# Window attention into a SiLU MLP: the first eight pairs' P times V in float32, with V whole in SBUF

## The chip, the cores and the metric

The kernel runs on one NeuronCore of a Trainium2 chip, in one launch. The metric is device time in microseconds (us) of that core. Before the change the median of three runs is 961.42 us (960.21 to 961.59).

## The reference

Eight batches of eight heads, 576 positions, head dimension 64, all in float32. Attention looks back over a window of 128 positions with a linear bias per head; its output, 4608 tokens of 512 features, goes through a SiLU MLP with 2048 hidden features.

```python
scores = scale * np.matmul(q, k.transpose(0, 1, 3, 2))
mask = (rel >= 0) & (rel < window)
scores = np.where(mask, scores + bias[None], -1000000000.0)
scores = scores - np.max(scores, axis=-1, keepdims=True)
attn = np.exp(scores)
attn = attn / (np.sum(attn, axis=-1, keepdims=True) + 1e-09)
out = np.matmul(attn, v)
x = out.transpose(0, 2, 1, 3).reshape(B * S, H * D)
h = x @ w_in
g = h * (1.0 / (1.0 + np.exp(-h)))
y = g @ w_out
```

## The kernel before

Two batches stand one after the other as 1152 rows, nine blocks of 128 (NBLK); there are 36 blocks. A **pair** p is one block i = p // 2 of query rows and one half q = p % 2 of the eight heads, so there are 72 pairs. A block attends to itself and to the block ahead of it (block 0 of a double batch to itself alone). Tokens go through the MLP in nine groups of four blocks (512 tokens); the first group needs the pairs 0 to 7 finished, and all later pairs are worked on while the MLP of an earlier group runs on TensorE.

A pair takes these steps. `scores`: products of q and k into two PSUM tiles (sp). `row_max`: on VectorE, adds the bias table `tab` and takes the row maximum (t, mx). `exps`: exponentials on ScalarE. Transposition of P, for the first eight pairs on TensorE into PSUM (`p_transpose_first`, pt), for later ones by DMA (`p_transpose`, hl from hr). Splitting P, scaled by 2048, into two float16 parts (hl): `p_hi_first` on ScalarE and `p_lo_first` on VectorE. `attend`: P times V (av), where V is split into two float16 parts as well (v1, v2, after multiplication by a power of two), so three products of float16 stand for one. A column of ones in v1 gives the row sum. `normalize` (L525 to L539) divides; for the first four blocks it writes x into float32 tiles (`early`), which `x_transpose` turns on TensorE (xp) and splits into xh (ScalarE) and xl (VectorE).

The power of two by which V is multiplied (`vsc`) comes from the maximum of |V| over the double batch: `vscale_load` fetches nine blocks, `vscale_reduce` takes each block's maximum (odd blocks on VectorE, even ones on ScalarE for the first double batch), `vscale_finish` joins them in three stages: a reduction (vcol), a transposition on TensorE (vt) with a few operations on one element, and a product that spreads the result (vs). `v_hi` and `v_lo` split V; for the first four blocks both run on GpSimd (L384, L392, L393).

The MLP's weights arrive as 64-bit words and are turned into float32 parts in SBUF, 16 slices of each matrix, 32 in all. `w_next_load` issues a slice's load (512 KB). `w_next` splits a slice: two operations on ScalarE (L712, L719), a join on VectorE (L724), a copy on ScalarE (L734), a subtraction on GpSimd (L128), and it orders one further load a step later. AHEAD loads are ordered beforehand. Three slices are split ahead of the MLP, the rest during its first group.

The order on every engine is written by hand: `put(point, fn, ...)` files a function under a step number; step 0 is the first half product of the MLP, and `at(p)` is the step at which pair p's scores stand. Pairs 0 to 7 are eight steps apart, from step -82 to -26. Each engine runs its instructions in that order, and SP issues all DMAs of the kernel in order too: one that waits for its tile holds back those behind it. Tiles with a common tag share memory: `rv` (two buffers) serves the V blocks to be split and the blocks whose maximum is taken for a later double batch; the tags in EARLY are those of late weight slices. `keep_warm(n)` puts n matmuls without a use on TensorE (into the last columns of an av tile).

Of the kernel before, what the change touches and what calls it, by code (L numbers as in the profile page):

```python
# [6 lines left out]
F32 = mybir.dt.float32  # L7
# [60 lines left out]
EARLY = ("w0_15", "w1_15", "w0_14", "w1_14", "w0_12", "w1_12", "w0_13")  # L68
AHEAD = 9
# [15 lines left out]
def tile_window_attention_then_silu_mlp(ctx, tc, qk, qk16, v, w_in, w_out, base8, out):  # L85
# [72 lines left out]

    def vscale_load(b, i):

        t = early_tile(XD + i) if b == 0 else pool.tile([P, DM], F32, tag="rv", bufs=2, name=f"vm{b}_{i}")
        nc.sync.dma_start(t, v[b, i * P : (i + 1) * P, :])
        vred.setdefault(b, {})[i] = t

    def vscale_reduce(b, i):
# [4 lines left out]
        if b == 0 and i < GT:  # L170
            rvs[i] = t

        if b > 0 or i % 2:
            nc.vector.tensor_reduce(m, t, axis=AX.X, op=ALU.max, apply_absolute_value=True)
        else:
            junk = pool.tile([P, DM], F32, tag="gt", name=f"vj{b}_{i}") if b == 0 else t
            nc.scalar.activation(junk, t, AF.Abs, accum_out=m)
# [199 lines left out]
    def load_v(i):  # L377
        b, j = divmod(i, NBLK)
        rvs[i] = pool.tile([P, DM], F32, tag="rv", bufs=2, name=f"rv{i}")
        nc.sync.dma_start(rvs[i], v[b, j * P : (j + 1) * P, :])  # L380
# [7 lines left out]
    def v_lo(i):  # L388
        rv = rvs.pop(i).rearrange("p (h d) -> p h d", h=H)
        if i < GT:  # L390
            vs = pool.tile([P, H, D], F32, tag="gl", name=f"vs{i}")
            nc.gpsimd.tensor_scalar(vs, rv, vsc[0][:, 0:1], 1.0, op0=ALU.mult, op1=ALU.mult)  # L392
            nc.gpsimd.tensor_sub(v2[:, i % VSLOTS], vs, v1[:, i % VSLOTS, :, 0:D])  # L393
            return
# [91 lines left out]
    def p_hi_first(p, u):  # L486
        n = 2 - blocks(p).start
        st[p]["hl"][u] = hl = pool.tile([P, 8, P], F16, tag="hl", bufs=4, name=f"hl{p}_{u}")
        hi = hl[:, : 2 * n].rearrange("p a c -> p (a c)")
        nc.scalar.activation(hi, st[p]["pt", u], AF.Copy, scale=PSCALE)  # L490

    def p_lo_first(p, u):
        n, hl = 2 - blocks(p).start, st[p]["hl"][u]
        hi, lo = (hl[:, a * 2 * n : (a + 1) * 2 * n].rearrange("p a c -> p (a c)") for a in range(2))
        nc.vector.scalar_tensor_tensor(
            out=lo, in0=st[p].pop(("pt", u)), scalar=PSCALE, in1=hi, op0=ALU.mult, op1=ALU.subtract
        )

    def attend(p):
# [3 lines left out]
        for u in range(2):  # L503
            hl = st[p]["hl"][u][:, : 4 * (2 - o0)].rearrange("p (a h o) r -> p a h o r", a=2, h=2)
# [56 lines left out]
    def x_transpose(cc):  # L561
# [4 lines left out]
        nc.vector.tensor_sub(xl[:, cc], xp, f32(xh[:, cc]))  # L566
# [222 lines left out]
    for p in range(NPAIR):  # L789
        i, q = divmod(p, 2)  # L790
        n = at(p)
        if p == 2 * GT - 1:
# [220 lines left out]
```

## Time and profile before

| | |
|---|---|
| median of three runs | 961.42 us (960.21 to 961.59) |
| the profiled execution's own time | 960.08 us |
| its span, first to last instruction | 958.3 us |
| TensorE (PE) matmul busy | 924.9 us (97%) |
| VectorE (DVE) busy | 662.7 us (69%) |
| ScalarE (ACT) busy | 562.2 us (59%) |
| GpSimd (POOL) busy | 144.4 us (15%) |
| moved by DMA | 123.83 MB, mean 129 GB/s |

The page gives busy times over the whole span; stages differ. The first 51 us hold pairs 0 to 7, with no MLP. From then to the end TensorE works on the MLP with the later pairs in between; the first store of the first group is issued at 180.0 us, and the first group is the stretch in which weights are split. How to read a row of the timeline: start and length in us, engine, line, operation, output and inputs by tile names, shape, how many were merged, and in brackets the idle time of the engine just before and what ended it. L numbers are lines of the kernel before.

### The profile page before, as it was taken

Reading aid. Unit: us, or ns where it says so; the run is one execution under the profiler, and the core shown is the slowest. Engines: PE = TensorE matmul, PEld = TensorE weight load, DVE = VectorE, ACT = ScalarE, POOL = GpSimd, SP = SyncE. Lnnn points to the kernel's source line nnn. Section 1 sums busy time; section 2 is a strip of 40 time slices with the busy share of each in tenths; the row PEclk is TensorE's granted clock in tenths of the full one; section 3 lists DMA queues with packets and bytes.
Section 4 is the critical chain, followed back from the end, with each engine's and each line's share of the span. In section 5 each row is a group of like instructions: output and inputs, shape, how many; then the busy total and the mean of one; then the engine's idle time right before and its main releaser. Section 6 shows DMA issues by size and latency. Waiting matters only on the chain.

```text
span 958.3 us, 17430 instructions
## 1 busy us (share of the span) xinstructions
PE 924.9 (97%) x6574; PEld 576.1 (60%) x6574; DVE 662.7 (69%) x1610; ACT 562.2 (59%) x1160; POOL 144.4 (15%) x129
## 2 busy tenths in 40 slices
PE   7888999999999999999999999999999999999998
PEld 5766777777787888655545555555455555554443
DVE  4776887545778888799778787777777777743222
ACT  4776887776556665666567765555555555532222
POOL 3234666212212122000000000000000000000000
PEclk8998999999999999999999999999999999999999
DMA  7939892424438773544577855454554555421001
GB/s 231 297 91 269 215 267 61 116 61 89 88 79 226 179 166 71 137 105 100 116 197 208 208 146 151 110 112 95 152 110 109 113 147 110 89 50 55 1 1 44
DMA packets 205972, 123.83 MB, mean 129 GB/s; under 512 B 168512, under 2 KB 176704, under 8 KB 205888
## 3 DMA queue, kind: packets, MB, share of 16 engines
q1 hardware_dynamic: 205888, 122.72, 52.1%
q8 instruction: 52, 0.85, 0.4%
q14 instruction: 32, 0.26, 0.1%
HBM read 72.88 MB, written 9.44 MB: 86 GB/s over the span
## 4 chain that ended last, share of the span: by engine, by line
PE 78%; DVE 3%; ACT 3%; issue 1%; POOL 1%; DMA 0%; ACTq 0%; DVEq 0%; POOLq 0%; SPq 0%
PE o L682 34%; PE h L616 29%; PE h L621 6%; PE av L512 4%; PE sp L413 3%; PE sp L420 2%; DVE gt L634 1%; ACT t L452 1%; DVE v L395 1%; POOL gl L128 1%; ACT gt L629 1%; ACT gh L642 0%; DMA vm<-v 0%; ACT hr L461 0%; ACT gh L644 0%
## 5 line engine op out<-in xcount | busy, mean ns | idle before, releaser
L682 PE MATMUL o<-w,gh 128*128 128x512 f16 (+1 forms) x1152 | 351.7, 387 | 1.8 <-ACT gh L642 1.8
L616 PE MATMUL h<-xt,w 128*128 128x512 f16 (+1 forms) x1536 | 310.6, 353 | 0.0
L629 ACT ACTIVATE gt<-h,gsc 128x512 f32<-128x512 f32 x112 | 77.0, 688 | 259.2 <-PE h L616 257.1
L682 PE MATMUL o<-w,gl 128*128 128x512 f16 (+1 forms) x576 | 221.7, 385 | 2.1 <-POOL gl L128 1.3
L616 PEld LDWEIGHTS <-w 128*128 128x128 f16 x1536 | 144.5, 98 | 125.8 <-issue 2.2
L634 DVE SCALAR_TENSOR_TENSOR gt<-gt,h 128x512 f32<-128x512 f32 x144 | 98.5, 684 | 122.0 <-ACT gt L629 121.7
L682 PEld LDWEIGHTS <-gh 128*128 128x128 f16 x768 | 74.8, 98 | 88.6
L452 ACT ACTIVATE t<-t,mx 128x256 f32<-128x256 f32 (+1 forms) x288 | 120.6, 486 | 6.4 <-DVE mx L442 6.3
L466 DVE SCALAR_TENSOR_TENSOR hr<-t,hr 128x512 f16<-128x512 f32 (+1 forms) x128 | 95.9, 751 | 26.7 <-ACT hr L461 26.0
L650 DVE SCALAR_TENSOR_TENSOR gl<-gt,gh 128x512 f16<-128x512 f32 x96 | 66.3, 691 | 51.1 <-ACT gh L644 48.7
L384 POOL TENSOR_SCALAR v<-rv,vsc 128x512 f16<-128x512 f32 x32 | 27.9, 872 | 434.6 <-DMA rv<-v 223.4
L621 PE MATMUL h<-xh,w 128*128 128x512 f32 x256 | 90.8, 408 | 1.0 <-DVE xl L566 1.0
L128 POOL TENSOR_TENSOR gl<-gt,gh 128x512 fp32r<-128x512 f32 x45 | 60.2, 1338 | 181.1 <-ACT gh L642 140.0
L682 PEld LDWEIGHTS o<-w,gh 128*128 128x128 f32 x384 | 69.9, 188 | 17.3 <-ACT gh L642 2.5
L461 ACT ACTIVATE hr<-t 128x512 f16<-128x512 f32 (+1 forms) x128 | 75.9, 598 | 5.7 <-DMA hl<-hr 5.7
L512 PEld LDWEIGHTS <-hl 128*128 128x128 f16 x1632 | 58.4, 98 | 25.6 <-issue 15.4
L644 ACT ACTIVATE gh<-gt 128x512 f16<-128x512 f32 x96 | 60.0, 625 | 22.4 <-DVE gt L634 21.4
L512 PE MATMUL av<-v,hl 128*128 128x65 f16 (+1 forms) x1632 | 62.8, 194 | 9.9 <-DVE v L395 5.6
L682 PEld LDWEIGHTS <-gl 128*128 128x128 f16 x384 | 37.6, 98 | 47.7 <-DVE gl L650 3.2
L442 DVE CUSTOM_DVE_ANT_0 t<-sp,tab,vsc 128x256 f32<-128x256 f32 (+1 forms) x144 | 58.6, 462 | 9.3 <-PE sp L413 8.8
L130 DVE SCALAR_TENSOR_TENSOR x<-xs,x 128x256 f16<-128x256 f32 x64 | 43.9, 686 | 23.8 <-ACT x L549 23.7
L621 PEld LDWEIGHTS h<-xh,w 128*128 128x128 f32 x256 | 48.5, 190 | 13.7 <-DVE xl L566 1.2
(125 smaller groups left out, 1034.8 us busy)
## 6 DMA issues: line engine op xcount, KB each, us to landing
r<-qk SPq DMA_DIRECT2D x36, 512.0 KB, 4.3
out<-ot SPq DMA_DIRECT2D x36, 256.0 KB, 2.5
qs<-qk SPq DMA_DIRECT2D x18, 512.0 KB, 5.1
wr<-w_in SPq DMA_DIRECT2D x16, 512.0 KB, 6.6
wr<-w_out SPq DMA_DIRECT2D x16, 512.0 KB, 6.7
rv<-v SPq DMA_DIRECT2D x32, 256.0 KB, 3.2
vm<-v SPq DMA_DIRECT2D x27, 256.0 KB, 3.9
q<-qk SPq DMA_DIRECT2D x18, 256.0 KB, 3.2
```

The costliest lines, as they stand in the source:

```text
L128: engine.tensor_sub(out, a, b)
L452: nc.scalar.activation(x, x, AF.Exp, bias=st[p]["mx"][:, 2 * u + h : 2 * u + h + 1], scale=-1.0)
L461: nc.scalar.activation(split_of(p, u, hr)[:, 0], t[:, :, 2 * P - n :], AF.Copy, scale=PSCALE)
L466: nc.vector.scalar_tensor_tensor(out=hr[:, 1], in0=t[:, :, 2 * P - n :], scalar=PSCALE, in1=hr[:, 0], op0=ALU.mult, op1=ALU.subtract)
L512: nc.tensor.matmul(av[:, 2 * u + h, : rhs.shape[-1]], lhs, rhs, start=(n == 0), stop=(n == len(seq) - 1), skip_group_check=True,)
L616: nc.tensor.matmul(o, w[:, wp, cc], x, start=start and k == 0, stop=stop, skip_group_check=True)
L621: nc.tensor.matmul(hps[n], w[:, cc], x, start=(half == 0 and i == 0), stop=(half == 1 and i == len(seq) - 1), skip_group_check=True,)
L629: nc.scalar.activation(gt, hps[n], AF.Tanh, scale=scale)
L634: nc.vector.scalar_tensor_tensor(out=gt, in0=gt, scalar=1.0, in1=hps[n], op0=ALU.add, op1=ALU.mult)
L644: nc.scalar.activation(gh, gt, AF.Copy, scale=CUT)
L650: nc.vector.scalar_tensor_tensor(out=gl, in0=gt, scalar=CUT, in1=gh, op0=ALU.mult, op1=ALU.subtract)
L682: nc.tensor.matmul(ops[ti], a[:, t], w, start=(f == 0 and i == 0), stop=(f == NF - 1 and i == len(seq) - 1), skip_group_check=True,)
```

## The change

P times V of the pairs 0 to 7 takes float32: P is copied as it is from PSUM (`p_copy_first`, half of it on ScalarE, half on VectorE), and V of the first four blocks is loaded once, in float32, into tiles of its own with a column of ones (`load_whole`, vf). One float32 product takes the place of three float16 ones, without the V scale. The scale is worked out later, for block 3 (as the block ahead of block 4) and the blocks behind it; its reductions are spread over the pairs 3 to 7. The fillers inside the pairs go; 22 stand near the start. The loads of V blocks 4 to 8 for the maximum come among the weight loads, and blocks 4 and 5 stay in SBUF to be split from there (KEPT), not loaded again. AHEAD is 12 in place of 9. For later blocks `load_v` stands at n + 4, not n - 2. The splitting of V no longer has a form on GpSimd alone.

```diff
-EARLY = ("w0_15", "w1_15", "w0_14", "w1_14", "w0_12", "w1_12", "w0_13")
-AHEAD = 9
+EARLY = ("w0_12", "w1_11", "w1_15", "w1_14", "w0_15")
+WHOLE = ("w1_12", "w0_13", "w0_14", "w1_13")
+AHEAD = 12
+KEPT = 6
...
+    def load_whole(i):
+        vf[i] = t = pool.tile([P, H, D + 1], F32, tag=WHOLE[i], bufs=1, name=f"vf{i}")
+        nc.gpsimd.memset(t[:, :, D : D + 1], 1.0)
+        nc.sync.dma_start(t[:, :, 0:D], v[0, i * P : (i + 1) * P, :].rearrange("p (h d) -> p h d", h=H))
+        vred.setdefault(0, {})[i] = rvs[i] = t[:, :, 0:D]
...
     def v_lo(i):
-        rv = rvs.pop(i).rearrange("p (h d) -> p h d", h=H)
-        if i < GT:
-            vs = pool.tile([P, H, D], F32, tag="gl", name=f"vs{i}")
-            nc.gpsimd.tensor_scalar(vs, rv, vsc[0][:, 0:1], 1.0, op0=ALU.mult, op1=ALU.mult)
-            nc.gpsimd.tensor_sub(v2[:, i % VSLOTS], vs, v1[:, i % VSLOTS, :, 0:D])
-            return
+        rv = rvs.pop(i)
...
-    def p_hi_first(p, u):
-    def p_lo_first(p, u):
+    def p_copy_first(p, u):
         n = 2 - blocks(p).start
+        st[p]["hl"][u] = hl = pool.tile([P, 4, P], F32, tag="hl", bufs=4, name=f"hl{p}_{u}")
+        flat, pt = hl[:, : 2 * n].rearrange("p a c -> p (a c)"), st[p].pop(("pt", u))
+        if u:
+            nc.vector.tensor_copy(flat, pt)
+        else:
+            nc.scalar.copy(flat, pt)
...
         for u in range(2):
+            if p < 2 * GT:
+                for h in range(2):
+                    for o in range(o0, 2):
+                        nc.tensor.matmul(
+                            av[:, 2 * u + h], st[p]["hl"][u][:, h * (2 - o0) + o - o0], vf[i - 1 + o][:, 4 * q + 2 * u + h],
+                            start=o == o0, stop=o == 1, skip_group_check=True,
+                        )
+                continue
...
-            put(n + STEP + 1, keep_warm, 4)
+            for u in range(2):
+                put(n + STEP + 3, p_transpose_first, p, u)
+                put(n + STEP + 4, p_copy_first, p, u)
...
-        if p < 2 * GT:
-            put(a, keep_warm, 5)
-        z = a + (3 if p < 2 * GT else 1)
+        z = a + 1
...
+            if i >= KEPT:
+                put(n + 4, load_v, i)
...
-                put(n - 2, load_v, i)
-            put(a - 3, v_hi, i)
-            put(a - 2, v_lo, i)
+            if i == GT:
+                put(a - 5, v_hi, i - 1)
+                put(a - 4, v_lo, i - 1)
+            if i >= GT:
+                put(a - 3, v_hi, i)
+                put(a - 2, v_lo, i)
...
+        for i in (2, 3):
+            put(at(2 * i - 3) + 1, load_whole, i)
+        for i in range(GT, VCH):
+            put(at(4) + 3 + 3 * (i - GT), vscale_load, 0, i)
         for i in range(VCH):
-            put(at(0) + 3 + i // 2, vscale_reduce, 0, i)
+            put(at(3) + 6 + 4 * i, vscale_reduce, 0, i)
         for x in range(3):
-            put(at(0) + 8 + x, vscale_finish, 0, x)
+            put(at(7) + (6, 8, 16)[x], vscale_finish, 0, x)
         for n in range(AHEAD):
-            put(at(0) + 14 + 6 * n, w_next_load)
-        put(at(0) + 4, keep_warm, 10)
-        put(at(0) + 6, keep_warm, 10)
-        put(at(0) + 7, keep_warm, 6)
-        for n in (-25, -17, -10):
+            put(at(1) + 4 + 5 * n, w_next_load)
+        put(at(0) + 1, keep_warm, 6)
+        put(at(1) + 1, keep_warm, 16)
+        for n in (at(5) + 5, at(6) + 5, at(7) + 5):
             put(n, w_next)
```

Where the instructions stand now is seen best at three places. TensorE before, from the transposition of pair 7's P (pt7) to the start of pair 6's P times V (av6), with four fillers into av5 between:

```order
L484 MATMUL pt7_0_709<-ident_64,t7_0_644 128x128 x4
L484 MATMUL pt7_1_716<-ident_64,t7_1_684 128x128 x4
L150 LDWEIGHTS ident_64
L150 MATMUL av5_654<-ident_64 128x252
L150 LDWEIGHTS ident_64
L150 MATMUL av5_654<-ident_64 128x252
L150 LDWEIGHTS ident_64
L150 MATMUL av5_654<-ident_64 128x252
L150 LDWEIGHTS ident_64
L150 MATMUL av5_654<-ident_64 128x252
L512 LDWEIGHTS hl6_0_631
L512 MATMUL av6_730<-v1_67,hl6_0_631 128x65
```

The same place on TensorE in the changed kernel, from pair 6's transposition on:

```order
L495 MATMUL pt6_0_523<-ident_64,t6_0_441 128x128 x4
L495 MATMUL pt6_1_528<-ident_64,t6_1_444 128x128 x4
L237 MATMUL vt0_553<-ident_64,vcol0_544 1x128
L514 MATMUL av6_561<-vf2_154,hl6_0_535 128x65
L514 MATMUL av6_561<-vf3_260,hl6_0_535 128x65
L514 MATMUL av6_561<-vf2_154,hl6_0_535 128x65
L514 MATMUL av6_561<-vf3_260,hl6_0_535 128x65
L514 MATMUL av6_561<-vf2_154,hl6_1_537 128x65
L514 MATMUL av6_561<-vf3_260,hl6_1_537 128x65
L514 MATMUL av6_561<-vf2_154,hl6_1_537 128x65
L514 MATMUL av6_561<-vf3_260,hl6_1_537 128x65
L495 MATMUL pt7_0_574<-ident_64,t7_0_504 128x128 x4
```

The fillers are gone, pair 6's P times V is eight float32 products with the whole V (vf2, vf3), and the V scale's transposition vt0, which stood ahead of pair 2's scores, now stands right ahead of them. On ScalarE the changed kernel has, from pair 7's last exponentials to the first x part (wm0_1 and wr0_1 belong to the third weight slice, vj0_8 is |V| of block 8):

```order
L463 ACTIVATE t7_1_507<-t7_1_507,mx7_493 128x256 x2
L504 COPY hl6_0_535<-pt6_0_523 128x512
L730 ACTIVATE wm0_1_539<-wr0_1_232 128x512
L737 ACTIVATE wr0_1_232<-wr0_1_232 128x512
L192 ACTIVATE vj0_8_542,vmx0_287<-early4_414 128x512
L752 CAST w1_0_551<-wm0_1_539 128x512
L504 COPY hl7_0_586<-pt7_0_574 128x512
L580 CAST xh_69<-xp0_590 128x512
```

Block 8's |V|, which before stood ahead of every copy of P on this engine, stands behind a weight slice's first two operations. SP's queue began like this before (early2 to early6 hold the nine blocks of V, q, k, tab and wr are queries, keys, bias table and weight slices):

```order
L909 DMA tab_65<-base8 128x8x128
L162 DMA early2_102<-v 128x512 x2
L162 DMA early3_105<-v 128x512 x2
L162 DMA early4_108<-v 128x512 x2
L162 DMA early5_111<-v 128x512 x2
L162 DMA early6_114<-v 128x512
L375 DMA q1_116<-qk 128x512
L371 DMA k1_118<-qk 128x512
```

And in the changed kernel, from the fourth whole V block to just ahead of the ninth block of V:

```order
L172 DMA vf3_260<-v 128x8x64
L720 DMA wr2_0_281<-w_in 128x4x256
L725 DMA wr1_1_301<-w_out 128x1024
L178 DMA early2_337<-v 128x512
L720 DMA wr3_0_343<-w_in 128x4x256
L178 DMA early2_337<-v 128x512
L390 DMA q4_374<-qk 128x512
L386 DMA k4_376<-qk 128x512
L178 DMA early3_378<-v 128x512
L725 DMA wr2_1_386<-w_out 128x1024
L178 DMA early3_378<-v 128x512
L720 DMA wr4_0_412<-w_in 128x4x256
```

Block 8 (early4) follows behind the last of these rows. V's blocks for the maximum, which stood ahead of q1 and k1, now come among the weight loads; 28 transfers stand ahead of block 8's.

More of the change, by code (lines that the diff above doesn't have):

```diff
@@ L110, in tile_window_attention_then_silu_mlp, with early_part @@
     early = {}
-    def early_tile(n):
-        k, part = divmod(n, 2)
+    def early_part(k, part):
         if k not in early:
@@ L157, in tile_window_attention_then_silu_mlp @@
     vred = {}
+    vf = {}
+    def load_whole(i):
[3 more added lines that the diff above has]
+        vred.setdefault(0, {})[i] = rvs[i] = t[:, :, 0:D]
     def vscale_load(b, i):
-        t = early_tile(XD + i) if b == 0 else pool.tile([P, DM], F32, tag="rv", bufs=2, name=f"vm{b}_{i}")
+        t = early_tile(i) if b == 0 else pool.tile([P, DM], F32, tag="rv", bufs=2, name=f"vm{b}_{i}")
         nc.sync.dma_start(t, v[b, i * P : (i + 1) * P, :])
-        vred.setdefault(b, {})[i] = t
+        vred.setdefault(b, {})[i] = t = t.rearrange("p (h d) -> p h d", h=H)
+        if b == 0 and i < KEPT:
+            rvs[i] = t
     def vscale_reduce(b, i):
@@ L169, in vscale_reduce @@
         m = vred[b]["m"][:, i : i + 1]
-        if b == 0 and i < GT:
-            rvs[i] = t
         if b > 0 or i % 2:
-            nc.vector.tensor_reduce(m, t, axis=AX.X, op=ALU.max, apply_absolute_value=True)
+            nc.vector.tensor_reduce(m, t, axis=AX.XY, op=ALU.max, apply_absolute_value=True)
         else:
-            junk = pool.tile([P, DM], F32, tag="gt", name=f"vj{b}_{i}") if b == 0 else t
+            junk = pool.tile([P, H, D], F32, tag="gt", name=f"vj{b}_{i}")
             nc.scalar.activation(junk, t, AF.Abs, accum_out=m)
@@ L515, in attend @@
                     )
-    xt, whole, now = {}, [], [0]
+    xt, xps, whole, now = {}, {}, [], [0]
     def normalize(p, stage):
@@ L565, in x_transpose, with x_low @@
         nc.scalar.copy(xh[:, cc], xp)
-        nc.vector.tensor_sub(xl[:, cc], xp, f32(xh[:, cc]))
+        xps[cc] = xp
+    def x_low(cc):
+        nc.vector.tensor_sub(xl[:, cc], xps.pop(cc), f32(xh[:, cc]))
     def x_dma(i):
@@ L909, in tile_window_attention_then_silu_mlp @@
         nc.sync.dma_start(tab[:, :, P:], base8[:, :, P:])
-        for i in range(VCH):
-            vscale_load(0, i)
+        load_whole(0)
         load_q(1)
@@ L947, in tile_window_attention_then_silu_mlp @@
                     x_transpose(half)
+                    x_low(half)
                     continue
```

46 lines of the change are left out of this document (20 added, 26 removed).

## The prediction

> **What bounds the kernel now.** I read the page first, for the span and its closing chain.
>
> ```profile
> span 958.3 us, 17430 instructions
> ...
> PE 78%; DVE 3%; ACT 3%; issue 1%; POOL 1%; DMA 0%; ACTq 0%; DVEq 0%; POOLq 0%; SPq 0%
> ```
>
> The chain of work that ended last is TensorE to 78%, so what counts is when its long MLP stream begins and how often that stream halts. The busy times by stretch (PE, PEld, DVE, ACT, POOL, then granted clock, DMA share, GB/s) say where it is not full.
>
> ```profile
> 0.00:10.00 10.00, 8.46 (x66) 6.46 (x66) 1.62 (x9) 4.10 (x10) 0.99 (x8) 1.00 0.81 242
> 10.00:20.00 10.00, 4.38 (x26) 3.65 (x27) 6.14 (x29) 4.74 (x15) 3.08 (x4) 0.72 0.95 311
> ...
> 40.00:50.00 10.00, 5.64 (x82) 4.71 (x80) 5.49 (x12) 5.64 (x13) 5.27 (x5) 1.00 0.97 334
> 50.00:60.00 10.00, 8.47 (x51) 6.21 (x49) 7.25 (x21) 6.04 (x12) 1.27 (x1) 1.00 0.02 8
> 51.30:172.00 120.70, 110.64 (x726) 85.92 (x727) 92.21 (x209) 94.47 (x185) 69.70 (x50) 0.97 0.71 179
> ```
>
> There are holes at 10 to 20 and at 40 to 50 us, both ahead of the MLP, and 10.1 us of idle TensorE from 51.3 to 172. TensorE's timeline names them (start, length, tile; in brackets the idle time before it and who ended it).
>
> ```profile
> 4.54 0.71 PE L420 MATMUL sp<-k,q 64*128 64x128 f32 x8
> ...
> 14.45 0.37 PE L222 MATMUL vt<-ident,vcol 128*1 128x128 f32 x1 [4.63 <-DVE vcol L218]
> ...
> 16.47 2.08 PE L420 MATMUL sp<-k,q 64*128 64x128 f32 x16
> ...
> 32.77 1.16 PE L420 MATMUL sp<-k,q 64*128 64x128 f32 x16
> 33.86 1.09 PE L484 MATMUL pt<-ident,t 128*128 128x128 f32 x8
> 34.79 0.59 PE L150 MATMUL av<-ident 128*128 128x252 bf16 x4
> 35.22 0.89 PE L512 MATMUL av<-v,hl 128*128 128x65 f16 x24
> 35.95 0.70 PE L150 MATMUL av<-ident 128*128 128x252 bf16 x5
> 36.58 1.16 PE L420 MATMUL sp<-k,q 64*128 64x128 f32 x16
> ...
> 46.91 0.76 PE L512 MATMUL av<-v,hl 128*128 128x64 f16 x20 [1.99 <-POOL v L393]
> ...
> 51.30 0.50 PE L621 MATMUL h<-xh,w 128*128 128x512 f32 x1 [0.96 <-DVE xl L566]
> ...
> 56.08 0.50 PE L621 MATMUL h<-xh,w 128*128 128x512 f32 x1
> ```
>
> TensorE first waits 4.63 us for the maximum of all nine V blocks (vcol), because the float16 V needs its scale; pair 2's scores start only at 16.47. Then each pair takes 3.81 us (32.77 to 36.58) without a gap: scores 1.09, transposes 0.93, four fillers 0.43, P times V 0.73, five fillers 0.63. At the end P times V waits for the float16 split of V on GpSimd (46.91), and the MLP starts at 51.30, its second half at 56.08.
>
> **The change, part by part.** *The V scale leaves the path.* The first eight pairs read V unscaled, so pair 2's scores follow the opening alone. That is 4.54, two scores of half size (2 x 0.55), 22 fillers at 0.108 and half a set of transposes (0.46): 8.5, instead of 16.47.
>
> *P times V in float32.* The eight matmuls of a full pair replace 24 in float16, and the nine fillers (1.06 us a pair) go. No row shows a float32 matmul of 65 columns. A float32 matmul leaves two records (16 for the eight of scores). Below, at the float16 rate (0.73 / 24 = 0.030 a record) the eight cost 0.5 us; above, at the rate of two scores side by side (1.09 / 8 = 0.136), 2.2. I take the row nearest to it, the transposition, which also loads 128 float32 weights (0.93 / 8 = 0.116 a record): 1.86. A pair is then 1.09 + 0.93 + 1.86 = 3.88 on TensorE, no quicker than the 3.81 before: the end of the fillers pays for float32. Fifty-six matmuls are affected, so the two ends move the start of the MLP by at most +2 and, since other engines take over, about -3 us.
>
> Those other engines, by the groups of operations of the first 60 us (busy, mean ns):
>
> ```profile
> L442 DVE CUSTOM_DVE_ANT_0 t<-sp,tab 128x256 f32<-128x256 f32 x28 | 10.3, 420 | 1.9 <-PE sp L420 1.9
> L452 ACT ACTIVATE t<-t,mx 128x256 f32<-128x256 f32 x24 | 10.2, 503 | 0.0
> ...
> L495 DVE SCALAR_TENSOR_TENSOR hl<-pt,hl 128x512 f16<-128x512 f32 x12 | 7.7, 682 | 0.0
> ...
> L490 ACT ACTIVATE hl<-pt 128x512 f16<-128x512 f32 x12 | 6.6, 595 | 6.1 <-PE pt L484 6.1
> ...
> L539 DVE TENSOR_TENSOR early<-av,r 128x256 f32<-128x256 f32 x8 | 3.4, 424 | 0.3
> L712 ACT ACTIVATE wm<-wr 128x512 f32<-128x512 f32 x5 | 3.3, 662 | 0.0
> L719 ACT ACTIVATE wr<-wr 128x512 int32<-128x512 uint32 x5 | 3.3, 660 | 0.0
> L177 ACT ACTIVATE vj<-early 128x512 f32<-128x512 f32 x5 | 3.1, 626 | 3.0 <-DMA early<-v 3.0
> ...
> L724 DVE SCALAR_TENSOR_TENSOR wm<-wm,wr 128x512 int32<-128x512 int32 x4 | 2.9, 723 | 3.1 <-ACT wr L719 3.1
> ...
> L174 DVE TENSOR_REDUCE vmx<-early 128x1 f32<-128x512 f32 x4 | 2.7, 686 | 3.7 <-DMA early<-v 3.7
> L734 ACT CAST w<-wm 128x512 fp32r<-128x512 f32 x3 | 1.9, 618 | 2.3 <-DVE wm L724 2.3
> ...
> L218 DVE TENSOR_REDUCE vcol<-vmx 128x1 f32<-128x9 f32 x1 | 0.2, 163 | 0.8 <-ACT vj L177 0.8
> ```
>
> VectorE has four row maxima (1.68), the normalisation (0.42 and two small ones) and now one copy of P (0.68) a pair: about 3.2, and 4.6 where a V maximum (0.69) and a slice's join (0.72) fall in. ScalarE has four exponentials (2.01) and one copy (0.60); in the cycles of pairs 4 to 6 also |V| (0.63) and a slice's three operations (0.66, 0.66, 0.62), 5.2 in all. So early pairs go at 3.9, and the last three lag on ScalarE. Pair 7's scores: 8.5, the two short cycles (2.5 and 3.0, since pairs 0 and 1 have one key block), three of 3.88, and 1 for hand-overs and VectorE: 26.6. With scores, P times V of pair 5 and transposes of pair 6 TensorE gets to 30.5.
>
> *A new wait replaces the old one.* vt, the transposition of the V scale, now stands in TensorE's queue ahead of pair 6's P times V, with everything up to the MLP behind it. It needs |V| of block 8, which on ScalarE stands behind a copy and two operations of a slice (0.60 + 0.66 + 0.66): at the earliest 32.4, with ScalarE's lag 33 to 34. It also needs block 8 landed. Ahead of it and with it in SP's queue go 21 transfers of 256 KB and 8 of 512 KB, 9.7 MB; 2.4 MB move by 10 us and then 311 to 334 GB/s, so it lands at 10 + 7.3 / 0.31 = 33.5. From there: |V| 0.63, vcol 0.16, vt 0.37, P times V 1.86, transposes 0.93, the eight x transposes like them 0.93, vs (a product as small as vt) 0.37, P times V 1.86, 7.1 in all, and hand-overs: the MLP starts at 41 instead of 51.3. **Gain 10.1 us.** The second half (46 instead of 56.1) follows likewise.
>
> *V whole is written in runs of 256 bytes.* The nearest row is tab, whose runs are as short, beside V's rows of 2 KB (issue to landing):
>
> ```profile
> DMA to landing us min/median/max: 4.2/5.1/5.9
> ...
> DMA to landing us min/median/max: 4.2/5.8/6.6
> ```
>
> The first line is tab's, the second that of V: no loss shows, so I price it at 0. The Trainium skill (DMA: Bandwidth & Descriptors, Specifications) puts line rate at 512 B and above; were the four whole loads half as fast below it (an estimate: 4 x 0.26 MB / 0.31 more), the MLP would start 3.4 us later, at 44.4, and the time be 952.7, still in my first case. The row of tab does not bear this out, though it is one transfer among others.
>
> *Twelve slices ahead, V's loads six steps later, V 4 and 5 kept.* In the MLP's first group, before:
>
> ```profile
> 70.20 0.34 SPq L380 DMA_DIRECT2D rv<-v  x1
> ...
> 73.10 4.05 SPq L474 DMA_TRANSPOSE hl<-hr  x1
> ...
> 82.58 0.63 ACT L461 ACTIVATE hr<-t 128x512 f16<-128x512 f32 x1 [4.56 <-DMA hl<-hr]
> ...
> 85.61 2.04 PE L420 MATMUL sp<-k,q 64*128 64x128 f32 x14 [4.69 <-DVE xs L539]
> ```
>
> SP reaches rv at 70.20 and then issues 2.1 MB at once; the transposition of P behind them (73.10) lands late, ScalarE waits 4.56, TensorE 4.69, and restarts at half rate (14 score records in 2.04 instead of 0.95). The change drops rv of blocks 4 and 5, and the idle DMA of 50 to 60 us is filled by slices ordered earlier. The stall with its slow restart is worth 6; it can go or move. I take **2 us** of it, bounds 0 and 6. Later the shift could cost: rv landed 2.7 to 4.7 us after its issue, and is needed by v_lo.
>
> ```profile
> DMA to landing us min/median/max: 2.7/3.2/4.7
> ...
> 620.57 2.62 SPq L474 DMA_TRANSPOSE hl<-hr  x2
> ...
> 626.61 0.75 DVE L395 SCALAR_TENSOR_TENSOR v<-rv,vsc,v 128x512 f16<-128x512 f32 x1
> ```
>
> Issued after the first of the two transpositions, at 621.9, it lands at 625.1, GpSimd adds 0.7, and VectorE asks at 626.6: just in time. A late one holds VectorE up to 1 us, some 3.5 us ahead of the attend it serves; I cost it at 0, at most 1 in all. The split of V 3 moves to VectorE in the first group (one operation of 0.75, beside 28 us of idle VectorE there).
>
> Sum: 10.1 + 2 = 12.1 off the profiled execution's own 960.08 (span 958.3 and 1.8 around it) is 948.0. The median shown is 1.3 above that execution, so I forecast **949.3**.
>
> **Rivals.** *A: the gain is partly given back.* The wait at vt grows (block 8 at 0.27 MB/us lands at 37), TensorE idles past 4 us, restarts at half rate as after 85.61 (about 2 us), and the first group keeps its stall: 10 - 3.5 - 2 = 4.5, so 957. For it: SP also waits for free q buffers. Against: the loads are queued well ahead of the DMA.
>
> *B: the loads are what set the MLP's start.* At the 242 GB/s of the first stretch throughout, block 8 lands at 40, the MLP starts near 48 with a slow restart and the first group, denser in DMA, loses 3 more: no change, 961. Against: 311 and 334 in the two stretches of full queues.
>
> *C, the slower side: without fillers the granted clock does not hold.* It fell after the 4.63 us hole (0.72 in 10 to 20). If it stays at half through the pairs, the 32 us from pair 2 to the MLP, 28 of them TensorE work, double to some 57: start at 66, and 961 + 15 - 1 = 975. It decides once the pairs' matmuls no longer count as busy. Against: from 40 to 50 us TensorE was busy 5.64 of 10, with gaps of 2 us, at clock 1.00; the new pairs fill more. The Trainium skill (TensorE: Matmul & The Clock Gate, Part 4: PE-mode transpose) says that transposes do not count as busy in the same way, which would leave 2.95 of each 3.88 us counted, more than the whole 5.64 of 10; the trace gives the rule no room to decide.
>
> *D: more.* The first group's stall goes entirely and float32 runs near its lower end: 17 off, 944.
>
> **How the numbers follow.** Forecast (944 to 953) 0.58, A 0.22, D 0.07, B 0.06, C 0.07. The range takes the forecast and A and leaves out C, B and most of D: 943.5 to 957.5. Faster by over 0.2% (1.9 us, about what a measurement of this kernel can tell from no change): 0.58 + 0.22 + 0.07 = 0.87; same 0.06; slower 0.07.
>
> **What would show it.** Pair 2's scores near 8.5 us; pairs 3.9 us apart; a wait before vt at 31 to 35 us, ended by VectorE's vcol; the MLP's first matmul at 41; clock 1.00 from 10 to 30 us; fewer than 10 us of idle TensorE over the first group. I am wrong if float32 P times V takes over 2.2 us a pair, if the clock falls among the pairs, or if the first group loses more than it did.

## The result and the profile after

| | before | after |
|---|---|---|
| median, us | 961.50 (960.21 to 961.63, 4 runs) | 951.95 (949.61 to 952.30, 4 runs) |
| ratio to before, 95% interval | | 0.9898 (0.9880 to 0.9916) |
| the profiled execution's own time | 960.08 | 949.61 |

The change saves 1.0%. The profiled execution of the changed kernel is the quickest of its four, 2.3 us under the median; that matters below. The page's span and closing chain:

```profile
span 947.8 us, 17110 instructions
...
PE 78%; ACT 5%; DVE 5%; issue 2%; DMA 1%; POOL 1%; SPq 0%; DVEq 0%; ACTq 0%; POOLq 0%
```

The chain is still TensorE to 78%, with a little more of ScalarE and VectorE in it. TensorE's timeline at the points that the prediction named (start, length, operation; in brackets the idle time before, and who ended it), L numbers now those of the changed kernel:

```profile
8.95 1.53 PE L431 MATMUL sp<-k,q 64*128 64x128 f32 x16
...
19.98 1.16 PE L431 MATMUL sp<-k,q 64*128 64x128 f32 x16
21.66 2.00 PE L514 MATMUL av<-vf,hl 128*128 128x65 f32 x16 [0.52 <-ACT hl L504]
23.49 1.04 PE L495 MATMUL pt<-ident,t 128*128 128x128 f32 x8
24.47 1.16 PE L431 MATMUL sp<-k,q 64*128 64x128 f32 x16
...
28.96 1.16 PE L431 MATMUL sp<-k,q 64*128 64x128 f32 x16
...
32.58 1.04 PE L495 MATMUL pt<-ident,t 128*128 128x128 f32 x8
37.26 0.27 PE L237 MATMUL vt<-ident,vcol 128*1 128x128 f32 x1 [3.64 <-DVE vcol L233]
37.37 2.58 PE L514 MATMUL av<-vf,hl 128*128 128x65 f32 x16
39.74 1.91 PE L495 MATMUL pt<-ident,t 128*128 128x128 f32 x8
...
45.14 0.48 PE L639 MATMUL h<-xh,w 128*128 128x512 f32 x1
...
49.48 0.50 PE L639 MATMUL h<-xh,w 128*128 128x512 f32 x1
...
75.22 1.13 PE L431 MATMUL sp<-k,q 64*128 64x128 f32 x14 [0.94 <-DVE xs L554]
```

Pair 2's scores went from 16.47 to 8.95. Pairs 3 and 4 follow after 2.94 and 3.60 us, and from pair 4 on pairs are 4.49 us apart; from pair 3's scores on, each P times V waits 0.52 or a little more for ScalarE's copy of P. Then comes a hole (idle time) of 3.64 ahead of vt, and after it a transposition takes 1.91 instead of 1.04. The MLP starts at 45.14 (51.30 before), its second half at 49.48 (56.08). In the first group the stall of 4.69 has become one of 0.94.

The busy times by stretch (PE, PEld, DVE, ACT, POOL, then granted clock, DMA share, GB/s), the last one from the second half of the first product to the first store's issue, which took 123.96 us before:

```profile
20.00:30.00 10.00, 8.96 (x97) 8.18 (x96) 8.20 (x34) 8.04 (x19) 1.28 (x1) 1.00 1.07 373
30.00:40.00 10.00, 5.74 (x46) 5.39 (x44) 6.61 (x25) 7.48 (x17) 2.37 (x2) 0.93 1.05 378
40.00:50.00 10.00, 9.36 (x66) 7.73 (x65) 4.85 (x12) 2.83 (x5) 0.17 (x1) 0.90 0.74 277
49.48:169.85 120.37, 112.47 (x748) 87.40 (x747) 96.08 (x222) 98.92 (x193) 68.67 (x50) 1.00 0.63 159
```

The clock is 1.00 among the pairs, falls after the hole, and stays at 1.00 over the first group. The 10.5 us between the two profiled spans (958.3 and 947.8) are 6.6 up to the second half of the first product, 3.6 in the first group (123.96 to 120.37), and 0.3 behind it.

The hole is told by ScalarE's timeline ahead of vt. Its last rows are pair 7's exponentials, the copy of pair 6's P, two operations of the third weight slice, and then |V| of block 8:

```profile
33.11 1.71 ACT L463 ACTIVATE t<-t,mx 128x256 f32<-128x256 f32 x4
34.72 0.57 ACT L504 COPY hl<-pt 128x512 f32<-128x512 f32 x1
35.19 0.66 ACT L730 ACTIVATE wm<-wr 128x512 f32<-128x512 f32 x1
35.75 0.65 ACT L737 ACTIVATE wr<-wr 128x512 int32<-128x512 uint32 x1
36.29 0.63 ACT L192 ACTIVATE vj<-early 128x512 f32<-128x512 f32 x1
```

No wait stands before |V| of block 8: ScalarE's queue set vt, not the load. SP issues block 8 at 27.39, and the loads of blocks 4 to 8 landed 6.7 to 7.4 us after their issue, so it was there by 34.8. And the 4.49 us per pair are told by VectorE's second half of the row maxima, which needs one of three t tiles, which are used in turn (a ring), and gets it when TensorE has transposed an earlier one:

```profile
19.76 0.42 DVE L453 CUSTOM_DVE_ANT_0 t<-sp,tab 128x256 f32<-128x256 f32 x1 [1.68 <-PE pt L495]
```

Its exponentials, and the copy of P behind them on ScalarE, are late by that. So three questions go to the chip: what the hole, the slow clock and the ring of t cost; which part of the change brought the 3.6 us of the first group; and whether the gain comes from the V scale's move or from float32.

### The profile page after: what moved, and what is told of

It is laid out like the page before. It is cut to its first block, busy times and chain, and to the rows that moved or that the text cites. A ratio compares the mean times of both kernels' runs of the same rounds, so it can differ in the third digit from the quotient of the medians.

```text
span 947.8 us, 17110 instructions
## 1 busy us (share of the span) xinstructions
PE 921.9 (97%) x6442; PEld 574.9 (61%) x6442; DVE 655.0 (69%) x1603; ACT 558.9 (59%) x1152; POOL 133.5 (14%) x122
## 4 chain that ended last, share of the span: by engine, by line
PE 78%; ACT 5%; DVE 5%; issue 2%; DMA 1%; POOL 1%; SPq 0%; DVEq 0%; ACTq 0%; POOLq 0%
PE o L700 34%; PE h L634 29%; PE h L639 6%; PE av L527 4%; PE sp L424 3%; PE sp L431 2%; DVE wm L742 1%; ACT t L463 1%; DVE t L453 1%; DVE gt L652 1%; ACT gt L647 1%; DVE x L137 1%; ACT wr L737 1%; ACT hr L472 1%; DVE v L406 1%
## 5 line engine op out<-in xcount | busy, mean ns | idle before, releaser
L400 POOL TENSOR_SCALAR v<-rv,vsc 128x512 f16<-128x512 f32 x30 | 24.4, 814 | 446.1 <-DMA rv<-v 233.1
L527 PEld LDWEIGHTS <-hl 128*128 128x128 f16 x1464 | 51.8, 98 | 22.4 <-issue 13.0
L527 PE MATMUL av<-v,hl 128*128 128x65 f16 (+1 forms) x1464 | 55.8, 193 | 7.1 <-DVE v L406 5.7
L453 DVE CUSTOM_DVE_ANT_0 t<-sp,tab 128x256 f32<-128x256 f32 (+1 forms) x144 | 50.5, 401 | 13.4 <-DMA tab<-base 7.1
```

Of the source, the lines that this page charges most:

```text
L453: nc.vector.tensor_tensor_reduce(out=t[:, h, 2 * P - n :], in0=st[p]["sp"][h][:, u, o].rearrange("p o c -> p (o c)"), in1=tab[:, 4 * q + 2 ...
L527: nc.tensor.matmul(av[:, 2 * u + h, : rhs.shape[-1]], lhs, rhs, start=(n == 0), stop=(n == len(seq) - 1), skip_group_check=True,)
```

## The experiments

The opening differs between executions (pair 2's scores at 8.95 to 10.17 in kernels that are alike up to there), so the runs are compared by two stretches: from pair 2's scores to the MLP's first product, and from its second half to the first store's issue. Each stretch is read from the one profiled execution of its kernel. The changed kernel's 36.2 is on the low side: five kernels with the same work on the engines up to the MLP (four below with an edit of the first group undone, and V in rows of 2 KB, which differs in V's loads) took 37.0 to 37.1. So what is counted from 36.2 below may be up to 0.9 too small.

| kernel | pair 2's scores | MLP starts | between | first group | median, us | ratio to before (95%) |
|---|---|---|---|---|---|---|
| before | 16.47 | 51.30 | 34.8 | 124.0 | 961.50 | |
| after | 8.95 | 45.14 | 36.2 | 120.4 | 951.95 | 0.9898 (0.9880 to 0.9916) |
| scale behind pair 7 | 9.05 | 43.87 | 34.8 | 120.8 | 949.94 | 0.9873 (0.9852 to 0.9894) |
| fillers ahead of vt | 9.64 | 44.92 | 35.3 | 120.0 | 951.05 | 0.9884 (0.9866 to 0.9902) |
| six t tiles | 10.10 | 44.39 | 34.3 | 120.7 | 950.06 | 0.9873 (0.9854 to 0.9893) |
| six t tiles, scale behind pair 7 | 9.02 | 40.82 | 31.8 | 121.1 | 946.40 | 0.9834 (0.9812 to 0.9857) |
| tail cleared as well | 9.31 | 37.71 | 28.4 | 120.6 | 943.91 | 0.9828 (0.9797 to 0.9859) |
| tail cleared further | 9.70 | 37.71 | 28.0 | 121.5 | 945.20 | 0.9837 (0.9822 to 0.9853) |
| AHEAD 9 | 10.16 | 47.20 | 37.0 | 120.0 | 952.43 | 0.9908 (0.9885 to 0.9932) |
| load_v at n - 2 | 10.03 | 47.02 | 37.0 | 120.2 | 953.29 | 0.9915 (0.9888 to 0.9942) |
| KEPT 4 | 9.83 | 46.83 | 37.0 | 122.8 | 953.85 | 0.9917 (0.9892 to 0.9943) |
| these three together | 10.17 | 47.24 | 37.1 | 125.4 | 957.22 | 0.9959 (0.9941 to 0.9977) |
| scale first, float32 kept | 16.97 | 53.45 | 36.5 | 120.8 | 959.67 | 0.9977 (0.9966 to 0.9988) |
| V in rows of 2 KB | 9.27 | 46.31 | 37.0 | 120.5 | 951.81 | 0.9908 (0.9892 to 0.9924) |

**The V scale behind pair 7.** Stages 2 and 3 of the scale go behind the MLP's first steps.

```diff
-            put(at(7) + (6, 8, 16)[x], vscale_finish, 0, x)
+            put(at(7) + (6, 27, 29)[x], vscale_finish, 0, x)
```

> The changed kernel, with stages 2 and 3 of the V scale (vt and vs) put behind pair 7's P times V, at steps 1 and 3 of the MLP. In the changed kernel TensorE idled 3.64 us ahead of vt (37.26), and the matmuls behind it ran slowly (clock 0.93 and 0.90 from 30 to 50 us); the MLP started at 45.14. Theory: the wait is that of vt for |V| of block 8 on ScalarE, and the slow matmuls come from that hole. Then pair 6's P times V starts when its copies of P are there, near 35.9 instead of 37.37, the clock stays at 1.00, and the MLP starts at 41.3 (1.5 of wait and 2.3 of slow work less); time 3 to 4 us less than the changed kernel. Rival: pair 6's P times V is held by the copies of P themselves and the hole stays long enough for the clock to fall: 1.5 less at most, MLP start at 43.6 or later.

TensorE at pair 6's P times V in this kernel:

```profile
35.19 3.60 PE L514 MATMUL av<-vf,hl 128*128 128x65 f32 x16 [1.71 <-ACT hl L504]
```

The wait is now for ScalarE's copy and half as long, but the product takes 3.60 instead of 2.00: the clock fell all the same. Of the 3.64 us hole 1.9 went, and 1.4 of that came through. The start at 43.87 is what the rival had (43.6 or later, with the clock falling), not the 41.3 of the theory. By the ratios' intervals this kernel can't be told apart from the changed one.

**Fillers ahead of vt.** Matmuls without a use keep TensorE busy in the hole.

```diff
         put(at(1) + 1, keep_warm, 16)
+        put(at(7) + 7, keep_warm, 24)
```

> The changed kernel, with 24 fillers (2.6 us) between pair 6's transposition and vt, inside the hole of 3.64 us. Theory: the slow matmuls from 37.4 to 43 (P times V 2.4, transposes 1.7, x transposes 1.5, where 1.83, 0.98 and 0.97 would be the pace) follow from the idle time: with the fillers the clock stays at 1.00, vt still starts at 37.3, and the MLP starts 2.0 to 2.5 us earlier, near 42.9. Rival: the clock falls from the few matmuls of the whole stretch, or those matmuls are slow for another reason: MLP start unchanged within 0.5 us of 45.1.

TensorE, then the two stretches, in this kernel:

```profile
35.69 2.74 PE L157 MATMUL av<-ident 128*128 128x252 bf16 x24 [1.62 <-DVE early L554]
...
38.58 1.97 PE L514 MATMUL av<-vf,hl 128*128 128x65 f32 x16
...
30.00:40.00 10.00, 7.72 (x74) 6.86 (x71) 7.15 (x25) 7.92 (x18) 2.35 (x3) 1.00 1.06 381
40.00:50.00 10.00, 9.23 (x72) 7.65 (x72) 4.97 (x13) 2.79 (x5) 0.60 (x1) 1.00 0.69 257
```

The clock stays at 1.00 beside the same DMA traffic (381 GB/s), and P times V takes 1.97: it was the clock that made these matmuls slow, not the transfers. The fillers write into av5's tile, so they waited 1.62 us for its normalisation and then made vt itself late; what they saved they mostly spent, 0.9 us being left of it in the stretch. So the theory's cause held, but not its start at 42.9 (44.92 came), and the time is not told apart from the changed kernel's.

**Six t tiles.** The second halves of the first eight pairs' t take idle weight tiles.

```diff
+        if p < 2 * GT and u:
+            t = pool.tile([P, 2, DM], F32, tag=("w0_10", "w1_9", "w0_11")[p % 3], bufs=1, name=f"t{p}_{u}")
+            t = t[:, 0].rearrange("p (h c) -> p h c", h=2)
+        else:
+            t = pool.tile([P, 2, 2 * P], F32, tag="t", bufs=3, name=f"t{p}_{u}")
```

> The changed kernel, with three more buffers for the tiles t of the pairs 0 to 7 (in the memory of late weight slices), so six instead of three. In the changed kernel pairs were 4.49 us apart where 3.88 was forecast: P times V waited 0.52 us in each pair for ScalarE's copy of P, which stands behind exponentials, and VectorE's second half of row maxima waited 0.8 to 1.7 us a pair for TensorE's transposition to free a t tile. Theory: the ring of three t tiles sets the pace; with six the waits of VectorE for the transposition go, pairs come 3.9 us apart, pair 7's scores start near 26 instead of 28.96, and the MLP starts up to 3 us earlier. Rival: the row maxima's wait costs nothing and ScalarE's order alone delays the copy: still 4.5 us a pair.

TensorE in this kernel, two pairs' scores and the hole:

```profile
15.69 1.16 PE L431 MATMUL sp<-k,q 64*128 64x128 f32 x16
...
19.59 1.16 PE L431 MATMUL sp<-k,q 64*128 64x128 f32 x16
...
35.52 0.37 PE L237 MATMUL vt<-ident,vcol 128*1 128x128 f32 x1 [3.63 <-DVE vcol L233]
```

Pairs are 3.90 apart, as first predicted (3.88), so the ring of three is what made them 4.49. The hole stays as long, and the start follows by 1.9 us in the stretch; the two ratios' intervals overlap here too.

**Both.** The two edits in one kernel.

> Both: six buffers for t, and vt and vs behind pair 7's P times V. If the two waits are independent, the gains add: MLP start near 38.5 (45.1 less 3.8 and 3), 6 to 7 us less than the changed kernel. Rival: ScalarE, with 5.2 us of work in each of the pairs 4 to 6, takes over, and it starts at 41 or later. If the loads of the weights come too late for an earlier start, the first group of the MLP grows by what the start gains.

TensorE at pair 6's P times V, the MLP's start, and the stretch of the hole:

```profile
33.77 2.35 PE L519 MATMUL av<-vf,hl 128*128 128x65 f32 x16 [1.71 <-ACT hl L509]
...
40.82 0.48 PE L644 MATMUL h<-xh,w 128*128 128x512 f32 x1
...
30.00:40.00 10.00, 8.29 (x60) 7.59 (x59) 6.52 (x21) 7.60 (x17) 2.54 (x2) 0.83 1.06 379
```

The two together take 4.4 us off the stretch (1.9 and 1.4 alone) and 5.6 off the median (1.9 and 2.0 alone), and by the intervals this kernel is faster than the changed one. That it is more than the sum isn't shown: behind the same wait of 1.71, P times V took 2.35 here and 3.60 with the scale alone, so about 1.2 us of it is how the clock fell in this one execution. ScalarE still holds pair 6's P times V back by 1.71, as the rival had it (a start at 41 or later, 40.82 came), and the clock still falls.

**The tail cleared.** In addition, the maxima of V blocks 6 to 8 and the third slice's split go behind the transposition of x, the first two slices one pair earlier.

```diff
-            put(at(3) + 6 + 4 * i, vscale_reduce, 0, i)
+            put(at(3) + 6 + 4 * i if i < 6 else at(7) + (9, 15, 20)[i - 6], vscale_reduce, 0, i)
-            put(at(7) + (6, 8, 16)[x], vscale_finish, 0, x)
+            put(at(7) + (24, 27, 29)[x], vscale_finish, 0, x)
-        for n in (at(5) + 5, at(6) + 5, at(7) + 5):
+        for n in (at(4) + 5, at(5) + 5, at(7) + 16):
```

> Six t tiles and the V scale behind pair 7, as in the fourth run (946.4), and in addition the maxima of V blocks 6 to 8 behind the transposition of x, the first two slices split one pair earlier and the third behind the transposition of x, so that ScalarE has only exponentials and copies of P among pairs 6 and 7. Theory 1 (ScalarE's queue sets the holes ahead of pairs 5 and 6's P times V, and the holes the clock): holes of under 1 us, granted clock 1.00 from 20 to 45 us, MLP's start 2 to 3 earlier than 40.82, time 943.5 to 945. Theory 2 (loads, or the spacing of 3.90 us on TensorE, set the pairs): the start moves by under 1, time 945.5 to 947. Theory 3 (what is moved is late for the first products, since the slice splits and x wait on the same engines): start earlier but the second half of the first product not, time 946 to 948.

TensorE in this kernel, and its stretch from 30 to 40 us:

```profile
28.73 2.00 PE L519 MATMUL av<-vf,hl 128*128 128x65 f32 x16 [0.97 <-ACT hl L509]
...
31.85 2.00 PE L519 MATMUL av<-vf,hl 128*128 128x65 f32 x16 [0.24 <-ACT hl L509]
...
37.71 0.48 PE L644 MATMUL h<-xh,w 128*128 128x512 f32 x1
...
40.12 0.50 PE L644 MATMUL h<-xl,w 128*128 128x512 f32 x1 [1.23 <-DVE xl L589]
...
30.00:40.00 10.00, 8.36 (x67) 7.28 (x66) 6.52 (x19) 6.38 (x14) 0.55 (x1) 1.00 1.06 382
```

The first theory held: holes under 1 us, clock 1.00, the start 3.1 us earlier than in the last kernel, at the same 380 GB/s. This kernel has the lowest median of the study, 943.91 (943.71 to 946.88); by the ratios' intervals it isn't told apart from the one before it (0.9828 and 0.9834), so the step rests on the profile. A wait of 1.23 for xl was left, which on VectorE stood behind a maximum and a join.

**The tail cleared further.** The third slice and the maxima of blocks 7 and 8 a few steps later still.

```diff
+            put(at(3) + 6 + 4 * i if i < 6 else at(7) + (9, 22, 21)[i - 6], vscale_reduce, 0, i)
+        for n in (at(4) + 5, at(5) + 5, at(7) + 23):
```

> As the run with the cleared tail (943.9), with the third slice's split and the maxima of V blocks 7 and 8 moved a further 2 to 7 steps, behind the second x part. There TensorE still waited 1.23 us for xl, which on VectorE stood behind a slice's join and a maximum. Theory 1: that wait goes, the second half of the first product starts at 41.3 to 41.8 instead of 42.77, time 942.5 to 943.2. Theory 2 (the slice is then late for the second product or the scale for block 3's split): the gain is given back in the first 10 us of the MLP, time 943.5 to 945.

TensorE in this kernel, where the second product comes in:

```profile
48.66 0.74 PE L705 MATMUL o<-w,gh 128*128 128x512 f32 x2 [0.93 <-ACT gh L665]
50.17 0.52 PE L705 MATMUL o<-w,gl 128*128 128x512 f32 x1 [0.77 <-POOL gl L135]
...
51.90 2.08 PE L431 MATMUL sp<-k,q 64*128 64x128 f32 x16
```

A miss: the wait for the first xl fell to 0.54, but the second half of the first product stands at 42.81, as before (42.77), since TensorE then waited 0.66 ahead of vt, for the next xl. That xl waited for ScalarE's xh (41.43), which now stood behind the copy of the moved slice (L757 at 40.91, itself 2.38 late behind the slice's join on VectorE). The scores behind two short holes ran at half speed (2.08); the kernel before this one has the same two holes (0.92 and 0.73) and ran them at 1.16. The median, 945.20, lies above the first theory's range and just above the second's, and the runs of the two kernels overlap.

**One edit of the first group undone at a time, then all three.**

```diff
-AHEAD = 12
+AHEAD = 9
```

> Only AHEAD goes back from 12 to 9. Measured so far: from the second half of the first product to the first store's issue the changed kernel takes 120.3 us, before 123.9, and a stall of 4.69 us became one of 0.94. Theory 1 (the three slices ordered earlier fill the idle DMA ahead of the group and relieve SP's queue): that stretch goes back to about 124, a stall of over 4 us behind a late transposition of P returns, time 951 + 3.5 = 954.5. Theory 2 (the dropped and shifted V loads did it): the stretch stays at 120 to 121, time within 1 of 951.

```diff
-                put(n + 4, load_v, i)
+                put(n - 2, load_v, i)
```

> Only load_v goes back from n + 4 to n - 2, for all blocks from 6 on. Theory 1 (the order of V's loads and the transpositions of P in SP's queue is what removed the stall): the first group's stretch grows from 120.3 to 122 or more and the time by 2 to 3. Theory 2 (the shift is worth nothing there): within 1 of 951. For the later groups the prediction said 0, at most 1 lost by the shift: if so the rest of the span, 778.0 from the first store, shrinks by up to 1.

```diff
-KEPT = 6
+KEPT = 4
```

> Only KEPT goes from 6 to 4: V blocks 4 and 5 are loaded a second time for the split, as before (0.5 MB more, two more transfers in SP's queue in the first group). Theory 1 (the burst of transfers behind which the transposition of P landed late is what the change removed): the stall of 0.94 us near 75 us grows to 3 or more, the first group's stretch from 120.3 to 122.5 to 124, time 953 to 955. Theory 2 (not the burst): within 1 of 951.

> All three edits of the first group are undone together: AHEAD 9, KEPT 4, load_v at n - 2. One by one they measured, from the second half of the first product to the first store's issue, 120.0 (AHEAD 9), 120.2 (n - 2) and 122.8 us (KEPT 4), against 120.3 with all three edits in and 123.9 in the kernel before. Theory 1 (they act together, through the burst of transfers in SP's queue): 123.5 to 124.5, and a stall of over 3 us behind one late transposition of P. Theory 2 (only the second loads of blocks 4 and 5 count): 122.5 to 123, and the last 1.1 us came from elsewhere.

The first group's stretch with KEPT 4 alone, then in the kernel with all three undone the stretch and TensorE's stall, with SP's and ScalarE's rows that lead to it:

```profile
51.17:173.94 122.77, 112.75 (x747) 86.91 (x746) 96.15 (x220) 98.98 (x193) 69.28 (x50) 1.00 0.65 160
...
51.58:176.94 125.36, 113.23 (x747) 88.38 (x746) 96.61 (x220) 98.96 (x193) 68.62 (x50) 0.97 0.69 169
...
67.22 0.34 SPq L395 DMA_DIRECT2D rv<-v  x1
...
69.50 2.71 SPq L485 DMA_TRANSPOSE hl<-hr  x1
...
79.08 0.63 ACT L472 ACTIVATE hr<-t 128x512 f16<-128x512 f32 x1 [4.08 <-DMA hl<-hr]
...
81.51 2.04 PE L431 MATMUL sp<-k,q 64*128 64x128 f32 x14 [5.11 <-DVE xs L554]
```

AHEAD 12 and the later V loads are worth nothing alone (120.0 and 120.2 us against 120.4), so both first theories fall there. The second loads of blocks 4 and 5 cost 2.4, but spread over waits of TensorE of at most 1.5 us, not as the stall that was expected: one transposition of P landed 6.3 us after its issue and held ScalarE for 3.42, TensorE for 0.8. With all three undone the stall of 5 us is back, with scores at half speed behind it, and the stretch is 5.0 longer. Its cause is the one named in the prediction: SP reaches rv at 67.22 and issues five transfers in a row, the transposition behind them lands 9.5 us after its issue (9.4 in the kernel before, 3.0 to 3.8 in the changed one from 58 to 82 us), and ScalarE waits 4.08 for it. So the edits act together: with any one of them undone the other two still keep the large stall away. Why 125.4 is 1.4 more than the kernel before had wasn't tried.

**The scale first, float32 kept.** V's nine loads and the whole scale ahead of pair 2's scores.

```diff
-        load_whole(0)
+        for i in range(GT):
+            load_whole(i)
+        for i in range(GT, VCH):
+            vscale_load(0, i)
...
+            put(at(0) + 3 + i // 2, vscale_reduce, 0, i)
+            put(at(0) + (8, 11, 13)[x], vscale_finish, 0, x)
```

> Float32 P times V stays, but all nine loads of V and the whole V scale go back ahead of pair 2's scores, as before the change. Theory 1 (the gain at the MLP's start comes from taking the scale off the path, the float32 form only makes that possible): a hole of 4 us or more ahead of vt, pair 2's scores at 15 to 17 instead of 8.95, no hole ahead of pair 6's P times V, so the MLP's start at 46 to 48 and its second half at 50.5 to 52, time 953 to 956. Theory 2 (the float32 form with its fewer operations is itself worth 4 or more of it): start at 44 or earlier, time 951 or less. A start near 51 would say that the whole gain hangs on the scale.

TensorE in this kernel, then two stretches:

```profile
14.66 0.37 PE L237 MATMUL vt<-ident,vcol 128*1 128x128 f32 x1 [5.06 <-DVE vcol L233]
...
16.97 2.08 PE L431 MATMUL sp<-k,q 64*128 64x128 f32 x16
...
47.59 2.00 PE L514 MATMUL av<-vf,hl 128*128 128x65 f32 x16 [1.70 <-ACT hl L504]
...
53.45 0.48 PE L639 MATMUL h<-xh,w 128*128 128x512 f32 x1
...
10.00:20.00 10.00, 3.89 (x24) 3.38 (x25) 5.09 (x23) 4.15 (x13) 0.00 (x0) 0.63 1.09 358
20.00:30.00 10.00, 10.00 (x62) 8.89 (x62) 5.05 (x22) 3.90 (x10) 0.00 (x0) 0.52 0.56 178
```

The hole is back, and the MLP starts at 53.45, later than before the change (51.30): with the scale on the path nothing of the gain at the start is left. But neither theory had so late a start, nor 959.67, nor the wait of 1.70 ahead of pair 6's P times V. A part of it is the clock: from pair 2's scores to the end of pair 2's P times V this kernel took 14.31 us (16.97 to 31.28), the changed one 10.05 for the same operations (8.95 to 19.00). At that pace the MLP would start 4.3 earlier, near 49.2 (an estimate). So the run shows that the gain at the start needs the scale off the path; what float32 is worth by itself stays open. What is left of the gain in time, 0.23%, fits the first group (120.8 against 124.0) less the later start. TensorE, busy without a gap from 20 to 30 us, was still granted about half the clock. The kernel before had such a hole too (4.63 us), but its pairs had their fillers, and in the same stretch its clock was nearly back:

```profile
20.00:30.00 10.00, 10.00 (x138) 8.72 (x135) 8.44 (x33) 6.94 (x17) 4.32 (x6) 0.94 0.50 156
```

That would fit fillers being of use behind a hole. It isn't shown: the two kernels also differ in the type of P times V and in the size of the hole, no run put fillers back into the pairs, and in the changed kernel the clock came back without them, about 6 us behind the hole of 3.64.

**V in rows of 2 KB.** The four whole blocks are loaded contiguously, and GpSimd spreads them.

```diff
-        nc.sync.dma_start(t[:, :, 0:D], v[0, i * P : (i + 1) * P, :].rearrange("p (h d) -> p h d", h=H))
+        nc.sync.dma_start(raw, v[0, i * P : (i + 1) * P, :])
+        nc.gpsimd.tensor_copy(t[:, :, 0:D], raw.rearrange("p (h d) -> p h d", h=H))
```

> The four whole blocks of V are loaded in rows of 2 KB into tiles of their own and spread by GpSimd, idle there, into the form with the column of ones; all else as in the changed kernel. Theory 1 (runs of 256 bytes cost nothing here, as priced): the loads of V take as long as before from issue to landing (5.9 us median), the tab and block 8 land within 0.5 us of the changed kernel's, time within 1 of 951. Theory 2 (half the rate below 512 bytes): the 20 to 40 us stretch shows the same GB/s but block 8 lands up to 3.4 us earlier and the opening is up to 0.9 us quicker, time 950 or less. Against both, GpSimd's copy may hold pair 0's P times V by up to 1 us.

SP's issue of block 8, first in the changed kernel, then in this one:

```profile
27.39 0.33 SPq L178 DMA_DIRECT2D early<-v  x1
...
24.50 0.33 SPq L182 DMA_DIRECT2D early<-v  x1
```

The time is the same, 951.81, but SP reaches block 8 2.9 us sooner (1.8 to 2.9 against the changed kernel and the three with one edit undone, where it stands at 26.33 to 27.39). The four loads themselves landed 4.1 to 5.4 us after their issue (median 4.9), against 4.5 to 7.2 (5.9) in runs of 256 bytes, so the short runs were not free. The Trainium skill's rule of 512 B (DMA: Bandwidth & Descriptors, Specifications), by which I had estimated 3.4, fits that. The rate from 30 to 40 us (382 GB/s, 378 in the changed kernel) shows no loss, though, and the run doesn't separate slower transfers from longer work on each load in SP's queue. It costs no time because ScalarE's queue, not block 8, ends the wait at vt.

## Why the prediction was right, and where it was not

949.3 was forecast, 951.95 measured, inside the range and the first case. That it came so close is partly luck, since errors cancelled. Up to the second half of the first product the change gained 6.6 instead of 10.1, the first group gave 3.6 instead of 2 and what follows 0.3 instead of 0, so the profiled execution took 949.61 instead of 948.0; and the median lay 2.3 above it instead of 1.3.

*The scale leaves the path*: right, pair 2's scores at 8.95 (8.5 forecast), and the last but one experiment shows that without it nothing of the gain at the start is left.

*P times V in float32*: 1.83 us a pair (21.66 to 23.49), 1.86 forecast from the transposition's rate. The sum on TensorE was right too (3.90 apart with six t tiles). What failed is "So early pairs go at 3.9": they went at 4.49. I added up each engine's busy time and did not follow the ring of three t tiles, in which the maxima of a pair wait for a transposition that the change had moved two steps later. That is 0.6 us a pair.

*The new wait at vt*: it stands where and for whom it was named. But block 8's |V|, for which the prediction said "with ScalarE's lag 33 to 34", began at 36.29, and vt came 28.3 us after pair 2's scores instead of 25.8 (34.3 and 8.5). That too is the ring: with six t tiles it came after 25.4 (35.52 and 10.10). From vt to the MLP 7.9 us passed instead of 6.7, since the clock fell after the hole, which the sum had no term for: P times V took 2.58 instead of 2.00, the transpositions 1.91 and 1.61 instead of 1.04 and 1.15 (the last of these as with the tail cleared). Of the 3.7 us that the start was late by, counted from pair 2's scores, 2.5 are the ring and 1.2 the clock and hand-overs. In the four kernels whose engines do the same up to the MLP (AHEAD 9, load_v at n - 2, KEPT 4, all three) the stretch took 37.0 to 37.1, against 36.2 in the changed kernel's one profile; a whole P times V, not a part of it, ran slow there (3.58). Most executions of the changed kernel probably do the same, which would account for part of the 2.3 us by which its median lies above its profiled execution. The gain at the start was to be 10.1 and was 6.2.

*The first group*: 2 forecast between 0 and 6, 3.6 measured, and the mechanism, the burst of transfers ahead of a transposition of P, was right, as the kernel with all three edits undone shows. The stall nearly went, as case D had it. I took 2, far from the end of 6, since the stall could move; undone singly, no edit brings it back.

*256-byte runs at 0*: right for the time, but not for the reason given, that no loss shows: the loads landed later and SP reached block 8 later, and only ScalarE's queue hid it. A further change could take that cover away.

*The shift of V's loads later in the kernel*: 0, as forecast: 778.0 us behind the first store's issue, 778.3 before, and 778.7 with load_v back at n - 2.

Rival A came half true: its near-4 us hole and slow restart came (3.64), though by ScalarE's queue and not by a late block 8, and its stall in the first group did not. B fell (the load was not what vt waited for), and C fell here: the clock was 1.00 from 10 to 30 us without the fillers. The sign "if the clock falls among the pairs" did come behind the hole, for pair 6's P times V and pair 7's transposition. A long slow stretch as in C came with the scale first, 0.52 over 10 us of pairs without a gap; that the missing fillers are its cause wasn't tested.

## What to carry to other kernels

Moving a dependence off a path is worth the old wait less the next one: follow every tile ring and every engine's queue up to the new wait, not only busy sums. Here 8 us more by the medians lay in the order of small operations, in where the scale's last stages stand and in three more buffers, nearly what the change itself brought (9.5). When several edits aim at one stall, undo them together as well as singly, since those that are left may still prevent it.

## What was not expected of the hardware

The granted clock fell after holes of 3.64 and 5.06 us, but also with one of 1.71 (P times V 3.60), while one of 1.70 at the same place left P times V at 2.00 with the scale first. Two holes of 0.9 and 0.8 were followed by scores at 2.08 in one kernel and 1.16 in another; the kernel before had kept 1.00 over a wait of 1.99. The Trainium skill (TensorE: Matmul & The Clock Gate, Part 1: The HAM clock gate) lets it fall after an idle window of about 3.4 us, and says that the windows run freely, so that the same kernel shows different counts of slow matmuls. The long holes and the differences between like kernels (P times V 2.58 or 3.58 behind the same hole) agree with that; the falls after 1.71 and after two short holes do not follow from one idle window. Nor does the slow stretch with the scale first, where the clock stayed near half over more than 10 us of unbroken work. What decides there stays open.
